# Splitting the stores of the last block: halves by partition, the last one over two DMA queues

## The chip, the cores and the metric

The kernel runs on one core of one Trainium2 chip. Its time is the device time of one execution in microseconds (us); the time before is the median of five runs.

## What is computed

The reference is a light-weight convolution followed by a two-layer block with a leaky ReLU:

```python
def _attn_ref(x, weight):              # x (8, 4096, 192), weight (8 heads, 7 taps)
    w = softmax(weight, axis=-1)       # written out, with 1e-9 in the sum
    x_pad = concat([zeros(6 rows), x], axis=1)
    ...                                # out[b,s,h,g] = sum_k w[h,k] * x_pad[b,s+k,h,g]

def _moe_ref(x, w_in, w_out):          # x (32768, 192), w_in (192, 2048), w_out (2048, 192)
    h = x @ w_in
    g = np.maximum(0.01 * h, h)
    return (g @ w_out).astype(np.float32)
```

The output has 32768 rows of 192 float32 values, 25.2 MB.

## The kernel before

The eight sequences are taken in four pairs, and each pair in blocks of 512 positions, so there are 32 blocks of 2 x 512 rows. For one block: GpSimd's DMAs load x in bf16, SyncE's transposing DMAs put the channels on the partitions, VectorE applies the seven taps (L226, L232), TensorE multiplies by w_in (L494), ScalarE applies the leaky ReLU (L501), and TensorE multiplies by w_out. The second product of a block runs one block late, interleaved with the first product of the next one. The order of each engine's instructions is the order in which the kernel's Python writes them; no scheduler moves them.

The second product comes in two forms. For the blocks in the middle (`mm2_slot`, L574) the result lies transposed in PSUM; `evac_t` (L596) transposes it back on VectorE into a tile `o_t`, and four DMAs store a block (L610). For the first two blocks and for the last one (`mm2_one`, L511) the result comes out with 128 rows of the output on the partitions. The last block has nothing left to be interleaved with, and it is done after the main loop, in eight pieces of 128 rows:

```python
    for n in range(LAST, len(subs)):
        po[n] = psum_o.tile([128, D], FP32, name="po", tag="po")
        for fc in range(NFC):
            mm2_one(None, n, fc, fc == 0, fc == NFC - 1)
        evac_o(n)
```

Each piece is 16 matmuls into a bank of PSUM, then `evac_o(n)`: one copy on VectorE from PSUM into a tile `o_sb` in SBUF (L622), and one store of 128 rows x 768 bytes from SyncE's queue (L625 before). Below, pieces are numbered 1 to 8 and a piece's store has its number. Three things tie these steps to each other:

- Both pools rotate through four buffers (`po` in PSUM, `o_sb` in SBUF). So the copy of piece 5 writes the buffer that store 1 reads, and waits until that store has landed; pieces 6, 7 and 8 wait in the same way for stores 2, 3 and 4.
- The DMAs that SyncE and ScalarE issue signal their landing on eight semaphores, taken in turn, which the built program calls DMAHW0 to DMAHW7. A DMA is issued only when the previous one on its semaphore has landed. SyncE has four stores of `o_t` (L610) just ahead of the last block's stores. They take DMAHW0 to 3, stores 1 to 4 take DMAHW4 to 7, and stores 5 to 8 take DMAHW0 to 3 again.
- After its last store SyncE runs the program's end, which the profile puts on the line of the launch (L745): nine waits one after the other, each for one or two semaphores of DMAs and engines; then all engines meet at a barrier. The nine take the hardware queues' semaphores in this order: none, DMAHW0, 1, 2, 3, 4, 5, 6, 7. In the built program the order is the same before and after the change.

ScalarE issues one DMA in the whole kernel, the load of the convolution's weights at the start (L288). Its last work is the leaky ReLU of the last block.

Of the kernel before, what the change touches and what calls it, by code (L numbers as in the profile page):

```python
# [15 lines left out]
def kernel(  # L16
# [8 lines left out]
    nc = tc.nc  # L25
# [46 lines left out]
    out_rows = out.rearrange("(r s) d -> r s d", r=B)  # L72
# [226 lines left out]
    for sign, off in ((1, 0), (-1, GRP - 1)):  # L299
        nc.gpsimd.affine_select(  # L300
            out=sel[:, :, 0, :], in_=sel[:, :, 0, :], compare_op=mybir.AluOpType.is_ge,
# [42 lines left out]
    for h in range(2):  # L344
        cs = slice(h * NFC // (2 * RUN), (h + 1) * NFC // (2 * RUN))
        nc.gpsimd.dma_start(
            out=w_out.rearrange("p (c i) d -> p c i d", i=RUN)[:, cs],
            in_=moe_w_out.rearrange("(c p i) d -> p c i d", p=128, i=RUN)[:, cs],
# [7 lines left out]
    def warm(n, cols=HT):  # L356
# [10 lines left out]
        out=nmax, in_=w9[:, 0:K], axis=mybir.AxisListType.X,  # L367
# [3 lines left out]
        out=w9[:, 0:K], in_=w9[:, 0:K], func=mybir.ActivationFunctionType.Exp,  # L371
# [61 lines left out]
    for p in range(2):  # L433
# [10 lines left out]
        out=rsum, in0=wml[:, :, K:], scalar=1e-9, in1=whm[:, :, 0, K:],  # L444
# [6 lines left out]
    def act_scale(out, in_, scale):  # L451
# [23 lines left out]
    subs = [  # L475
        (b, e, t0 // 128 + n)
        for b, t0, T in groups[:NSW] for e in range(2) for n in range(T // 128)
    ]
    LAST = len(subs)
# [39 lines left out]
    def mm2_row_slot(q):  # L519

        p, fc = divmod(q, 2 * NFC)
        rnd, fc = divmod(fc, NFC)
        pair = (2 * p, 2 * p + 1)
        first, last = fc == 0, fc == NFC - 1
        if first and rnd == 0:
            for n in pair:
                po[n] = psum_o.tile([128, D], FP32, name="po", tag="po")
        for rt in range(2):  # L530
            ins = mm2_one(
                rt, pair[rt ^ rnd], fc, first and rnd == 0, last and rnd == 1
            )
            if first and rnd == 1:
                sync(ins, seal, "both row tiles have left these banks")
        if last and rnd == 0:
            seal_round(p, ins)
        if last and rnd == 1:
            evac_o(pair[0])

    def seal_round(p, ins):


        nonlocal seal
        if p == 0:
            seal = nc.scalar.copy(out=junk, in_=junk)
        else:
            seal = evac_o(2 * p - 1)
        sync(seal, ins, "between the rounds")
# [65 lines left out]
    def evac_o(n):  # L615
        b, e, s = subs[n]
        rp, st = divmod(b, NB)
        if n % 2 == 0 or n >= LAST:
            osb[n] = o_pool.tile([128, 2, D], FP32, name="o_sb")
        o_sb = osb[n if n >= LAST else n - n % 2]  # L620
        copy = nc.scalar.copy if b < NHALF else nc.vector.tensor_copy
        ins = copy(out=o_sb[:, n % 2, :], in_=po.pop(n))  # L622
        if n >= LAST:
            t0 = st * ST + s * 128
            nc.sync.dma_start(out=out_rows[2 * rp + e, t0 : t0 + 128, :], in_=o_sb[:, n % 2, :])  # L625
        elif n % 2 == 1:
            t0 = st * ST + (s - 1) * 128
            nc.sync.dma_start(
                out=out_rows[2 * rp + e, t0 : t0 + 256, :].rearrange("(c p) d -> p c d", p=128),
                in_=o_sb,  # L630
            )
        return ins
# [21 lines left out]
    for i, grp in enumerate(groups):  # L654
        blk, t0, T = grp
# [10 lines left out]
        for j in range(steps):  # L666
# [41 lines left out]
            if i == NSW and j == steps - 1:  # L708
                evac_o(LAST - 1)
                slot = NSW * NR * NFC  # L710
# [39 lines left out]
```

## Time and profile before

| what | value |
|---|---|
| time, median of 5 runs | 681.69 us (681.49 to 682.32) |
| time of the profiled execution | 681.49 us |
| its span from the first to the last instruction | 679.8 us |
| TensorE busy | 675.8 us, 99% of the span, at the full granted clock |
| VectorE, ScalarE busy | 481.1 us, 518.7 us |
| the last block's second product (L511) | 10.73 us, from 665.87 us |
| the last copy (L622) | 0.36 us, from 676.64 us |
| the last store's issue (L625) | 0.33 us, from 677.02 us |

The span starts at the profile's zero. The difference between the execution's time and its span, 1.69 us, lies outside the instructions. In the timeline a row is: start, duration, engine, line, operation, tiles, count; in brackets the idle time before it and what ended that. An engine's name with a q (SPq, ACTq) means its instruction queue, where DMAs are issued and semaphores waited for; SP is SyncE.

### The profile page before, as it was taken

The page shows a single profiled execution, that of the slowest core. Times are in us where ns is not written, and L with a number is a line of the kernel's source. Part 1 is how long each engine was busy: PE and PEld are TensorE (multiplying, and loading weights), DVE is VectorE, ACT ScalarE, POOL GpSimd, SP SyncE. Part 2 cuts the span into 40 slices and gives each one's busy share as a digit, 9 for nine tenths or more (in the row PEclk, how much of TensorE's full clock was granted, in tenths as well). Part 3 has the DMA queues.
Part 4 walks back from the last instruction along what each step waited for, and adds up shares of the span by engine and source line. Part 5 has one row for each costly group of instructions (what it writes and reads, how often), then busy time and mean ns, then how long its engine had stood idle before and what let it go on. Part 6 is the DMA issues. An engine that isn't in the chain of part 4 may idle for free.

```text
span 679.8 us, 27088 instructions
## 1 busy us (share of the span) xinstructions
PE 675.8 (99%) x12444; PEld 447.7 (66%) x12444; DVE 481.1 (71%) x811; ACT 518.7 (76%) x608; POOL 146.2 (22%) x205
## 2 busy tenths in 40 slices
PE   9999999999999999999999999999999999999998
PEld 6997666666666666666666666666666666666667
DVE  7989467766768666778667687667786676876612
ACT  7899777777777778777777877778777777777781
POOL 7455211122201222211222112222112220000000
PEclk9999999999999999999999999999999999999999
DMA  9999746656647656646556366565665573321123
GB/s 152 92 114 109 55 79 89 83 62 71 91 76 96 72 55 87 92 77 85 65 64 95 75 94 78 56 83 83 88 86 67 59 96 72 72 56 35 32 50 94
DMA packets 213826, 53.27 MB, mean 78 GB/s; under 512 B 209232, under 2 KB 213328, under 8 KB 213712
## 3 DMA queue, kind: packets, MB, share of 16 engines
q0 software_dynamic: 98752, 13.97, 30.4%
q1 hardware_dynamic: 114944, 37.57, 27.4%
q8 instruction: 97, 1.59, 1.0%
q14 instruction: 17, 0.14, 0.1%
q10 hardware_dynamic: 16, 0.00, 0.0%
HBM read 28.31 MB, written 25.17 MB: 79 GB/s over the span
## 4 chain that ended last, share of the span: by engine, by line
PE 99%; DVE 0%; issue 0%
PE ph L494 49%; PE acc L574 44%; PE po L511 5%; PE acc L257 1%; PE warm L358 1%; PE ptr L188 0%; PE ptr L179 0%; DVE o_sb L622 0%; PE warm L394 0%; PE wps L394 0%
## 5 line engine op out<-in xcount | busy, mean ns | idle before, releaser
L501 ACT ACTIVATE g<-ph 128x1024 bf16<-128x1024 f32 x512 | 496.6, 1021 | 140.2 <-PE ph L494 140.0
L232 DVE SCALAR_TENSOR_TENSOR yt<-xt,wk,yt 128x512 bf16<-128x512 bf16 (+1 forms) x582 | 381.0, 724 | 0.2
L494 PE MATMUL ph<-yt,w_in 64*64 64x512 bf16 (+2 forms) x6048 | 377.1, 369 | 0.0
L574 PE MATMUL acc<-g,w_out 64*64 64x512 bf16 x5568 | 339.9, 376 | 0.0
L494 PEld LDWEIGHTS <-w_in 64*64 64x64 bf16 (+1 forms) x6048 | 229.7, 131 | 102.8 <-issue 0.8
L574 PEld LDWEIGHTS <-w_out 64*64 64x64 bf16 x5568 | 178.6, 118 | 118.4
L99 POOL DMA_DIRECT2D x_bf<-in_x_dram x180 | 133.8, 768 | 411.0 <-DMA xt<-x_bf 408.9
L596 DVE STREAM_TRANSPOSE o_t<-acc 128x512 f32<-128x512 f32 x87 | 72.8, 876 | 181.9 <-PE acc L574 181.9
L511 PE MATMUL po<-w_out,g 64*128 64x192 bf16 (+1 forms) x640 | 36.8, 243 | 0.0
L511 PEld LDWEIGHTS <-g 64*128 64x128 bf16 (+1 forms) x640 | 32.6, 95 | 3.2 <-issue 0.4
L226 DVE TENSOR_SCALAR yt<-xt,wk 128x512 bf16<-128x512 bf16 (+1 forms) x97 | 29.8, 335 | 3.2 <-DMA xt<-x_bf 3.1
L584 ACT COPY junk<-junk 128x1 f32<-128x1 f32 x58 | 11.1, 192 | 4.1
L622 DVE COPY o_sb<-po 128x192 f32<-128x192 f32 x8 | 2.8, 356 | 6.8 <-PE po L511 4.2
L257 PE MATMUL acc<-xt,diag 64*64 64x256 bf16 x140 | 5.4, 272 | 0.0
L622 ACT COPY o_sb<-po 128x192 f32<-128x192 f32 x16 | 5.1, 324 | 0.3
L257 PEld LDWEIGHTS <-diag 64*64 64x64 bf16 x140 | 4.3, 106 | 1.4 <-DVE diag L413 0.7
L358 PE MATMUL warm<-const-bfloat16-1.0 128*128 128x512 bf16 (+3 forms) x12 | 4.3, 513 | 0.8 <-PEq L734 0.8
L152 POOL DMA_DIRECT2D x_half<-in_x_dram x6 | 4.3, 730 | 1.0 <-DMA x_rows<-in_x_dram 0.9
L358 PEld LDWEIGHTS <-const-bfloat16-1.0 128*128 128x128 bf16 x12 | 1.5, 138 | 2.5 <-issue 2.5
L148 POOL DMA_DIRECT2D x_rows<-in_x_dram x4 | 2.9, 728 | 0.0
L413 DVE TENSOR_TENSOR diag<-ident,whm 128x448 bf16<-128x448 bf16 (+1 forms) x5 | 2.6, 582 | 0.0
L421 ACT ACTIVATE diag<-ident,whm 128x64 bf16<-128x64 bf16 x10 | 2.5, 336 | 0.0
(47 smaller groups left out, 24.3 us busy)
## 6 DMA issues: line engine op xcount, KB each, us to landing
out_dram<-o_t SPq DMA_DIRECT2D x116, 192.0 KB, 4.6
x_bf<-in_x_dram POOLq DMA_DIRECT2D x180, 64.0 KB, 3.2
out_dram<-o_sb SPq DMA_DIRECT2D x8, 192.0 KB, 3.4
xt<-x_bf SPq DMA_TRANSPOSE x90, 3.8
w_out<-in_moe_w_out_dram POOLq DMA_DIRECT2D x2, 384.0 KB, 8.0
out_dram<-o_sb SPq DMA_DIRECT2D x8, 96.0 KB, 2.0
w_in<-in_moe_w_in_dram POOLq DMA_DIRECT2D x2, 256.0 KB, 4.7
x_nat<-in_x_dram SPq DMA_DIRECT2D x2, 192.0 KB, 2.5
```

The costliest lines, as they stand in the source:

```text
L99: ins = nc.gpsimd.dma_start(out=t[:, c, :, e, :], in_=src[2 * rp + e, :, :, c * CH : (c + 1) * CH],)
L226: lambda s=src, d=dst, c=c: nc.vector.tensor_scalar_mul(d, s, wk[:, c, 0:1])
L232: lambda s=src, d=dst, c=c, k=k: nc.vector.scalar_tensor_tensor(out=d, in0=s, scalar=wk[:, c, k : k + 1], in1=d, op0=mybir.AluOpType.mult, ...
L257: lambda k=k, p=p, a=a, ps=ps, to=to, acc=accs[e * apart]: nc.tensor.matmul(out=acc[to, :T], lhsT=diag[c][ps, p, k, :], rhs=xt[0][ps, c, a ...
L358: nc.tensor.matmul(out=wa[:, 0, 0:cols], lhsT=ones[:, 0:128], rhs=ones[:, 0:cols], start=True, stop=True,)
L494: nc.tensor.matmul(out=ph[m : m + M, e, i * T : (i + 1) * T], lhsT=w_in_of(f, e, c, m, m + M), rhs=y[ps, c, t0 : t0 + T], start=(c == chun ...
L501: act = nc.scalar.activation(out=g[blk][:, nf * u : nf * (u + 1), :, t0 : t0 + T], in_=ph.rearrange("p e (i t) -> p i e t", i=nf), func=my ...
L511: return nc.tensor.matmul(out=po[m], lhsT=g[b][ps, fc, e, s * 128 : (s + 1) * 128], rhs=w_out[ps, fc, :], start=start, stop=stop,)
L574: ins = nc.tensor.matmul(out=acc2[gi, r][e * CH : (e + 1) * CH, 0:T], lhsT=w_out_of(ps, fc, r), rhs=g[b][ps, fc, e, t0 : t0 + T], start=fi ...
L584: seal = nc.scalar.copy(out=junk, in_=junk)
L596: nc.vector.transpose(out=osb[gi, 0][:, 0 : T // GB, :, r], in_=acc2.pop((gi, r))[:, 0:T].rearrange("p (j k) -> p j k", k=GB),)
L622: ins = copy(out=o_sb[:, n % 2, :], in_=po.pop(n))
```

## The change

In the last block, `evac_o` cuts some stores into halves by partition. For pieces 1, 2 and 3 the store becomes two stores of 64 rows, both from SyncE's queue. For piece 8, the last, it becomes two stores of 64 rows, the first half from SyncE's queue and the second from ScalarE's. Pieces 4 to 7 keep one store each. The copies, the matmuls and everything before the last block are the same; 8 stores become 12.

```diff
         if n >= LAST:
             t0 = st * ST + s * 128
-            nc.sync.dma_start(out=out_rows[2 * rp + e, t0 : t0 + 128, :], in_=o_sb[:, n % 2, :])
+            end = n == len(subs) - 1
+            parts = 2 if n < LAST + 3 or end else 1
+            for h in range(parts):
+                ps = slice(h * 128 // parts, (h + 1) * 128 // parts)
+                (nc.scalar if end and h else nc.sync).dma_start(
+                    out=out_rows[2 * rp + e, t0 + ps.start : t0 + ps.stop, :],
+                    in_=o_sb[ps, n % 2, :],
+                )
```

In the built program the stores after the change take the semaphores so: the halves of 1, 2 and 3 DMAHW4 and 5, 6 and 7, 0 and 1; stores 4 to 7 DMAHW2 to 5; of store 8, ScalarE's half DMAHW6 and SyncE's half DMAHW7. The copies of pieces 5, 6 and 7 each wait for two halves where they waited for one store.

## The prediction

> **What bounds the kernel now.** I read the chain that ended last first, since it says which part of the span the edit can touch at all. On the page:
>
> ```profile
> PE 99%; DVE 0%; issue 0%
> PE ph L494 49%; PE acc L574 44%; PE po L511 5%; PE acc L257 1%; PE warm L358 1%; PE ptr L188 0%; PE ptr L179 0%; DVE o_sb L622 0%; PE warm L394 0%; PE wps L394 0%
> ```
>
> TensorE is the chain from end to end. The chain stops at the copy of piece 8, so what comes after is not in it. No instruction ahead of the last block differs, so everything up to about 670 us stays. The question is the tail. The timeline from 676.5 us has it:
>
> ```profile
> 676.27 0.33 PE L511 MATMUL po<-w_out,g 128*128 128x192 bf16 x2
> 676.64 0.36 DVE L622 COPY o_sb<-po 128x192 f32<-128x192 f32 x1 [0.96 <-PE po L511]
> 677.02 0.33 SPq L625 DMA_DIRECT2D out_dram<-o_sb  x1
> ```
>
> The copy ends at 677.00, store 8 is issued 0.02 us later, and the span ends at 679.8. So 2.8 us are left after the last copy, and only these can be shortened. The view of line 625 from 676.9 us gives the store's "DMA to landing" as 1.6 us, so it lands at 678.6. The DMA view of 677.8 to 678.4 us, in 40 slices of 0.015 us, shows its packets:
>
> ```profile
> DMA  0001527488959799887998749263301000000000
> ```
>
> They start in the fourth slice, about 677.85, and end in the 31st, about 678.26: 0.42 us. So the store's 1.6 us are 0.83 before the first packet, 0.42 of packets and 0.35 until SyncE knows. What follows is the program's end (L745). Its waits on SyncE, asked for in two windows, 677.3:678.6 and 678.62:678.95:
>
> ```profile
> L745 SPq EVENT_SEMAPHORE  x4: 28/28/28, 677.4 to 677.6; - x4
> ```
>
> ```profile
> L745 SPq EVENT_SEMAPHORE  x5: 28/28/28, 678.7 to 678.9; - x5
> ```
>
> Four of the nine waits are passed while the store is still on its way. The fifth is the one for DMAHW3, store 8's semaphore. It holds SyncE, 1.0 us by the view of waits ("SPq L745 <- DMA out_dram<-o_sb: 1.0, 1, 1.0"), and four more come after it, for stores landed long before. Windows of 0.05 us show one of the five starting each 0.06 us. So after the landing SyncE spends 4 x 0.06 = 0.24 us on waits that have nothing to wait for, and then the barrier.
>
> **Part one: the semaphores.** Three more stores ahead of store 8 move the rotation on by three, and the fourth extra DMA is store 8's own second half. The halves of store 8 now signal DMAHW6 and 7, and these are the last two of the nine waits. The seven before them are passed while the halves are on their way: 7 x 0.06 = 0.42 us, against the 1.2 us between the end of issue (677.36) and the landing. After the landing one wait is left if both land together, 0.06 us, or none if ScalarE's half is first. So 0.24 - 0.06 = 0.18 us is saved, up to 0.24. I take 0.18. This gain is the sure one: it follows from order alone.
>
> **Part two: store 8 in two halves.** The 0.83 us before the first packet is not per row. The first o_t store is another shape (512 runs of 384 bytes) and its issue takes 0.32 us against 0.33 here, so half the rows should not shorten it. The 0.42 us of packets could at best be halved if two queues feed the DMA engines twice as fast: -0.21 us. The busy share in the row above reads 7 to 9 tenths in the middle, so the engines are nearly full there and little can be fed faster. Against it stands the only place where both queues issue together, the kernel's start:
>
> ```profile
> 0.81 0.60 ACTq L288 DMA_DIRECT2D w<-in_weight_dram  x1
> 0.81 0.96 SPq L145 DMA_DIRECT2D x_nat<-in_x_dram  x2
> ```
>
> There ScalarE's issue took 0.60 us, which is 0.27 more than store 8's 0.33, and SyncE's two took 0.96 with a gap, some 0.45 each. If the later half pays the same, the landing is 0.27 us later. The bounds are therefore -0.21 and +0.27, and I take 0: the rows at both ends are about equally far from this store. ScalarE is idle when it is asked: its last leaky ReLU ends before 666, and its half waits for DMAHW6 (the first half of store 2, landed by about 674.5) and for the copy. So nothing is queued behind it but the barrier.
>
> The Trainium skill, page "DMA: Bandwidth & Descriptors", section "Rules for kernel authors", speaks against this part: for two transfers to disjoint partition halves it says "Don't bother", since both halves run on the same 16 DMA engines and serialize. By that rule the gain of the halves is nothing and the sum is part one alone; by the best reading of the row it would be 0.21 us more.
>
> **Part three: three more issues on SyncE.** Stores 1 to 4 are issued at 670.50, 671.65, 672.56 and 673.05 and take 1.06, 0.81, 0.40 and 0.40 us; the first two are slow while the o_t stores' data drains (their own issues grow from 0.32 to 1.13 us). The gaps between issues are about 0.1 us. Each extra half costs at least one more short issue with its gap, 0.33 + 0.1 = 0.43 us; part of it falls into the time when the queue is full anyway. Three make 1.3 us at the low price. At the high price a half costs what its whole costs now: 1.06 + 0.81 + 0.40 + 3 x 0.1 = 2.57 us. I take 1.3, since the issues are short as soon as the drain is over. Two things must absorb this:
>
> ```profile
> 674.39 0.62 DVE L622 COPY o_sb<-po 128x192 f32<-128x192 f32 x2 [2.61 <-DMA out_dram<-o_sb]
> ```
>
> The copy of piece 5 already waits 2.61 us for store 1 to land (670.50 + 3.8 = 674.3). That wait is off the path: TensorE has four banks and never writes a ninth piece, so a late copy delays no matmul. What counts is the copy of piece 8, which needs store 4 landed. Store 4 is issued at 673.05 and takes 2.0 to land, at 675.05; TensorE frees the copy at 676.64. The slack is 1.6 us, and 1.3 fits. The other cover is SyncE's queue: stores 5 to 7 are issued at 674.78, 675.20 and 675.70, the last done at 676.08, and store 8 needs the queue at 677.02, so 0.94 us is free. Stores 4 and 5 gate these: with 1.3 us store 4's issue ends at 674.75, just as store 5 wants the queue. So part three is hidden: 0. Without that cover it would cost what exceeds 1.6 us.
>
> The semaphores' reuse adds waits too: store 4 now needs the third o_t store landed, and store 5 the fourth. The DMA view gives a median of 4.8 us for these, issued at 668.49 and 669.27, so 673.3 and 674.1; both are ahead of the time when those stores are issued anyway. Cost 0.
>
> **The sum.** -0.18 + 0 + 0 = about -0.2 us. The profiled execution took 681.49, so it would take 681.3, with a span of 679.6. That execution was the fastest of the five; the median lies 0.2 above it, and the forecast for the median is 681.69 - 0.2 = 681.5 us. This is 0.03%. A measurement of this kernel can tell about 0.2% from no change, 1.36 us, so I forecast no change.
>
> **The rivals.**
>
> - The halves overlap fully: two queues feed the engines at once, the packets take 0.21 us, and ScalarE's half lands first. Then -0.24 - 0.21 = -0.45, 681.2 us. For it: the fill and the drain of the packet row take part of its 0.42 us. Against: its middle is nearly full.
> - The two queues hinder each other as at the start: +0.27 - 0.18 = +0.1, 681.8 us. For it: the 0.60 us issue. Against: two DMAs stood on SyncE there.
> - Slower: store 4 comes so late that the copy of piece 8 waits for it. Price: at 2.57 us, store 4 lands at 677.6 instead of 675.05, the copy starts at about 677.7 instead of 676.64, everything after moves by 1.05 us, less 0.2: 682.5 us. It decides once the three halves cost SyncE more than 1.6 us together. To be slower by over 0.2% they would have to cost 1.6 + 1.36 + 0.2 = 3.2 us. Against it: the issues of 0.40 us from 672.56 on.
> - The change does not do what it says: ScalarE's half signals or starts late and the semaphores' order saves nothing. Then about 681.7.
>
> A gain of over 0.2% would need half of the 2.8 us after the last copy, and no mechanism here reaches a quarter of it.
>
> **How the numbers follow.** My forecast (part one alone, halves neutral) 0.45; full overlap 0.2; the queues hinder each other 0.15; the late store 4 0.1; no effect 0.1. All five lie within 0.2%; what is left over is the spread of executions (681.49 to 682.32, 0.12%) and a late store that costs more than I allow. Hence 0.04 faster, 0.90 same, 0.06 slower. The range: down from full overlap, 681.2, by 0.3, since the fastest of the five runs lies 0.2 below their median and five are few, 680.9; up to the late store, 682.5, which also takes in the slowest of the five runs less 0.2.
>
> **What would show it.** In the profile after: seven of SyncE's waits at L745 before the landing and two after it; 2.6 us from the end of the last copy to the end of the span; ScalarE's issue of about 0.3 to 0.6 us at 677.0; the copy of piece 8 at 676.64 still freed by TensorE, not by a DMA. I am wrong if the copy of piece 8 waits for a store, if the last half lands later than 1.6 us after its issue, or if TensorE's matmuls at L511 take other than 10.7 us.

## The result, and the profile after

The changed kernel takes 682.43 us (median of 25 runs), the kernel before 681.60 us (45 runs). The medians differ by 0.83 us, slower; the ratio of the means is 1.0011, 95% interval 1.0006 to 1.0017. It is small, inside the 0.2% that was called no change, and clear of noise, on the other side of the forecast. The profiled execution took 682.33 us, its span 680.6 us.

The page's chain that ended last, by engine and by line, after the change:

```profile
PE 98%; DMA 1%; SPq 0%; ACT 0%; DVE 0%; issue 0%; DVEq 0%
PE ph L494 49%; PE acc L574 44%; PE po L511 4%; PE acc L257 1%; DMA out_dram<-o_sb 1%; PE warm L358 0%; SPq L629 0%; ACT xt L199 0%; PE ptr L188 0%; DVE o_sb L622 0%; PE ptr L179 0%; PE wps L394 0%; DVEq L622 0%
```

Before, TensorE was the chain to its end. Now the chain has stores of `o_sb` and SyncE's queue in it. The same chain from 660 us on, in order of time (start, duration, what):

```profile
670.36 1.06 SPq L629
...
672.59 0.54 SPq L629
...
673.17 3.81 DMA out_dram<-o_sb x2
...
677.11 0.36 DVE o_sb L622
```

The last copy is no longer freed by TensorE. It waits for a store, and that store stands behind the halves in SyncE's queue. The timeline says the same:

```profile
677.11 0.36 DVE L622 COPY o_sb<-po 128x192 f32<-128x192 f32 x1 [0.20 <-DMA out_dram<-o_sb]
677.50 0.55 ACTq L629 DMA_DIRECT2D out_dram<-o_sb  x1
```

SyncE's issues one by one (the timeline of SP, one window for each): the second half of store 1, both of store 2, both of store 3, and store 4.

```profile
671.46 1.03 SPq L629 DMA_DIRECT2D out_dram<-o_sb  x1
672.59 0.54 SPq L629 DMA_DIRECT2D out_dram<-o_sb  x1
673.17 0.59 SPq L629 DMA_DIRECT2D out_dram<-o_sb  x1
673.87 0.54 SPq L629 DMA_DIRECT2D out_dram<-o_sb  x1
674.46 0.59 SPq L629 DMA_DIRECT2D out_dram<-o_sb  x1
675.15 0.53 SPq L629 DMA_DIRECT2D out_dram<-o_sb  x1
```

The halves of stores 2 and 3, 64 rows each, take longer to issue (0.54 to 0.59 us) than the whole store 3 did before:

```profile
672.56 0.40 SPq L625 DMA_DIRECT2D out_dram<-o_sb  x1
```

Two rows are something else. Store 1's second half takes 1.03 us, while the o_t stores' data is still draining, and store 4, which is whole, takes 0.53 behind a half.

The last store's two halves show "DMA to landing us min/median/max: 1.9/2.0/2.1", where the whole store showed 1.6. SyncE's half is the one that lands after 1.87 us, ScalarE's lands after 2.12. The DMA share from 678.4 to 679.4 us, in slices of 0.025 us, has the packets of both:

```profile
DMA  0000000003439479496556576795945311000000
```

Up to 678.89 the view counts packets of SyncE's queue alone. SyncE's first packet comes at 678.62, 1.13 us after the issue, and ScalarE's at 678.90, 1.40 us after it. A whole store took 0.83. Last, SyncE's waits of the program's end (L752 now), in the windows 678:679.6 and 679.6:679.76:

```profile
L752 SPq EVENT_SEMAPHORE  x7: 28/28/28, 678.0 to 678.6; - x7
L752 SPq EVENT_SEMAPHORE  x2: 28/28/28, 679.6 to 679.7; - x2
```

Seven before the landing and two after it, as forecast.

So the time can be split. Nothing before the last block differs, and still the copy of piece 1 starts at 667.33 us here and at 667.47 before; over all runs below it starts between 667.30 and 668.08. The rows, before and after:

```profile
667.47 0.36 DVE L622 COPY o_sb<-po 128x192 f32<-128x192 f32 x1
```

```profile
667.33 0.36 DVE L622 COPY o_sb<-po 128x192 f32<-128x192 f32 x1
```

I therefore count from that copy, which takes this spread out:

| stretch | before | after | difference |
|---|---|---|---|
| start of copy 1 to start of copy 8 | 9.17 | 9.78 | +0.61 |
| issue of store 8 until SyncE passes the wait for it | 1.63 | 2.14 | +0.51 |
| from there to the end of the span | 1.13 | 0.96 | -0.17 |
| start of copy 1 to the end of the span (the tail) | 12.32 | 13.27 | +0.95 |

Copy and wake-up between are the same. The tail's 0.95 less the 0.14 of earlier start is the 0.8 us by which the span grew.

### The profile page after: what moved, and what is told of

It is laid out like the page before. It is cut to its first block, busy times and chain, and to the rows that moved or that the text cites. A ratio compares the mean times of both kernels' runs of the same rounds, so it can differ in the third digit from the quotient of the medians.

```text
span 680.6 us, 27096 instructions
## 1 busy us (share of the span) xinstructions
PE 675.4 (99%) x12444; PEld 446.7 (66%) x12444; DVE 481.9 (71%) x811; ACT 518.8 (76%) x608; POOL 146.7 (22%) x205
## 4 chain that ended last, share of the span: by engine, by line
PE 98%; DMA 1%; SPq 0%; ACT 0%; DVE 0%; issue 0%; DVEq 0%
PE ph L494 49%; PE acc L574 44%; PE po L511 4%; PE acc L257 1%; DMA out_dram<-o_sb 1%; PE warm L358 0%; SPq L629 0%; ACT xt L199 0%; PE ptr L188 0%; DVE o_sb L622 0%; PE ptr L179 0%; PE wps L394 0%; DVEq L622 0%
```

## Experiments: which part costs what

The theory from this profile: the halves of stores 1 to 3 hold up store 4 and with it the copy of piece 8 (+0.6), the halves of store 8 land late (+0.5), the order of waits gives back 0.17. The rivals: two queues at once hinder each other; any three more DMAs cost this; the waits at the end are worth nothing. The times of each run stand with runs of the kernel before on the same chip; the tails are from the traces.

**Only the last store split.** `parts = 2 if end else 1`

> Only store 8 is split, over SyncE's and ScalarE's queues; stores 1 to 7 stay whole. If the loss has two parts, a late copy of piece 8 (0.6 us) and a late landing of the two halves (0.5 us), this keeps the second alone: the copy of piece 8 is freed by TensorE again, the last half lands 2.1 us after its issue instead of 1.6, and the kernel is 0.4 to 0.5 us slower than before. If the halves in SyncE's queue are the whole of it, the landing comes back to 1.6 us and the time is that of before, 0.06 us less for one wait fewer at the end.

682.19 us against 681.52, ratio 1.0009, interval 1.0000 to 1.0017. The tail is 12.91, +0.59.

```profile
677.09 0.36 DVE L622 COPY o_sb<-po 128x192 f32<-128x192 f32 x1 [0.96 <-PE po L511]
```

```profile
DMA to landing us min/median/max: 1.9/2.1/2.2
```

The copy is TensorE's again, the late landing stays. The second part exists alone. The tail's 0.59 is a little over the 0.4 to 0.5 that was expected.

**Only the first three split.** `parts = 2 if n < LAST + 3 else 1`

> Stores 1 to 3 are split, store 8 is whole on SyncE. With two parts of the loss: the copy of piece 8 waits for store 4 and starts 0.6 us later, store 8 lands 1.6 us after its issue, one wait follows instead of four (-0.18 us), in sum 0.4 us slower than before. If the two queues are the whole of the loss, the copy is on time and the kernel is 0.18 us faster than before.

682.13 us against 681.52, ratio 1.0009, interval 1.0000 to 1.0018. The tail is 12.66, +0.34, as expected; the whole time moved by 0.6, with an interval that holds both.

```profile
677.03 0.36 DVE L622 COPY o_sb<-po 128x192 f32<-128x192 f32 x1 [0.20 <-DMA out_dram<-o_sb]
```

Copy 1 is at 667.35 here, so copy 8 comes after 9.68. Store 8, whole again, lands after 1.6. The two parts' tails add up: 0.59 + 0.34 = 0.93, against 0.95 for the whole change.

**The order of the waits alone.** In the first two blocks four stores become two each, so the rotation moves on by four:

```diff
-            nc.sync.dma_start(out=out_rows[...].rearrange("(c p) d -> p c d", p=128), in_=o_sb)
+            parts = 2 if n >= LAST - 8 else 1
+            for h in range(parts):
+                cs = slice(h * 2 // parts, (h + 1) * 2 // parts)
+                nc.sync.dma_start(out=out_rows[...].rearrange(...)[:, cs], in_=o_sb[:, cs])
```

> The last block's stores are those of before; four stores of the first two blocks go in two halves by column of rows (128 rows each), which moves the rotation of semaphores on by four, so that store 8 signals DMAHW7, the last wait of the nine. If the order of the waits is worth what the prediction gave it, nothing but the barrier follows the landing: 0.24 us faster than before, eight waits ahead of the landing and one after it in the profile. If the waits at the end cost nothing, no difference.

The waits (L748) in the windows 677.4:678.7 and 678.7:678.82:

```profile
L748 SPq EVENT_SEMAPHORE  x8: 28/28/28, 677.5 to 677.9; - x8
L748 SPq EVENT_SEMAPHORE  x1: 28/28/28, 678.8 to 678.8; - x1
```

The tail is 12.09, -0.23: the size is right. The whole time does not show it: 681.63 against 681.52, ratio 1.0003, interval 0.9994 to 1.0012. A gain of 0.03% is below what these runs resolve, so it is shown in the trace alone.

## Experiments: two queues, or the half itself

**Store 8 whole on ScalarE's queue.** `(nc.scalar if n == len(subs) - 1 else nc.sync).dma_start(...)` in the kernel before.

> No store is split; store 8 goes whole to ScalarE's queue. If a half of 64 rows is slow by its form (in the changed kernel its first packet comes 1.1 us and more after the issue, where whole stores take 0.83), this whole store on the other queue has its first packet 0.83 us after its issue and lands after 1.6 us: the time of before. If ScalarE's queue is the slow one, it lands 0.3 to 0.5 us later and the kernel loses that.

681.54 us against 681.58, ratio 1.0000, interval 0.9991 to 1.0009. ScalarE's issue and its landing:

```profile
L625 ACTq DMA_DIRECT2D out_dram<-o_sb x1: 382/382/382, 677.1 to 677.1; - x1
...
DMA to landing us min/median/max: 1.7/1.7/1.7
```

ScalarE's queue is not slow: 0.05 us more issue than SyncE's, and its first packet comes 0.88 us after the issue instead of 0.83.

**Store 8 in halves of 64 rows, both on SyncE.** `parts = 2 if end else 1`, and `nc.sync` for both.

> Only store 8 is split, in halves of 64 rows, both on SyncE's queue. If the form is slow, the first half's first packet comes 1.2 us after its issue, as with two queues, the second half follows 0.64 us after the first as those of stores 2 and 3 do, and it lands 2.5 us after the copy: 0.8 us slower than before. If the two queues hinder each other, one queue frees the first half: its first packet comes after 0.83 us, and the second lands 2.1 us after the copy at most.

682.59 us against 681.58, ratio 1.0017, interval 1.0007 to 1.0026; the tail +0.93. The first half is issued at 676.86 and takes 0.56 us on a queue of its own. The DMA engines' busy share from 678 to 679.2 us, in slices of 0.03 us:

```profile
DMA  0033396939722100000000005376797842100000
```

The first packet comes at 678.07, 1.2 us after the issue, with no other queue at work. So a half is slow to start by itself. The pair of queues can still add to it; the next run has both queues without the 64 rows.

**Store 8 in halves by column over both queues.** Each half keeps 128 rows and has 384 bytes of each.

```diff
-                ps = slice(h * 128 // parts, (h + 1) * 128 // parts)
+                ds = slice(h * D // parts, (h + 1) * D // parts)
...
-                    in_=o_sb[ps, n % 2, :],
+                    in_=o_sb[:, n % 2, ds],
```

> Only store 8 is split, by column, 128 rows of 384 bytes each, over SyncE's and ScalarE's queues. If the form of 64 rows is slow and the queues do not hinder each other, both first packets come 0.83 us after the issue and the later half lands after 1.6 us: the time of before. If the two queues hinder each other, the later half's first packet comes 0.3 us or more after the other's, and it lands after 2.0 us or more.

681.63 us against 681.58, ratio 1.0002, interval 0.9993 to 1.0011; the tail 12.40, +0.08. The timeline, and the DMA share from 677.8 to 678.4 us in the slices of 0.015 us in which the prediction showed the whole store:

```profile
677.06 0.33 SPq L629 DMA_DIRECT2D out_dram<-o_sb  x1
677.06 0.38 ACTq L629 DMA_DIRECT2D out_dram<-o_sb  x1
```

```profile
DMA  0000002456788999999997998799886665231000
```

Both halves together are on the engines from 677.90 to 678.36, 0.46 us, where the whole store took 0.42. SyncE's first packet comes 0.84 us after its issue and ScalarE's 0.99, 0.15 us behind it, where ScalarE alone was 0.05 behind. So the two queues hinder each other by some 0.1 us, and they gain nothing either: the later half lands after 1.68 us. The rival is small here and not nothing. In the change ScalarE's half started 0.28 us behind SyncE's, and how much of this is the pair is open, as a half of 64 rows on ScalarE's queue alone was not run. The Trainium skill's page "DMA: Bandwidth & Descriptors", section "Rules for kernel authors", says of partition halves that they serialize on the same 16 engines; here neither cut gains, and the cut by partition loses 0.5 us besides.

**Stores 1 to 3 in halves by column.** As many DMAs as in the change, all on SyncE, store 8 whole.

> Stores 1 to 3 go in two halves by column, 128 rows of 384 bytes each, on SyncE; store 8 is whole. As many DMAs as with the halves by partition. If 64 rows are what makes a half dear, the issues after the first two take 0.33 to 0.40 us instead of 0.54 to 0.60, store 4 lands by about 676.0 at the latest, the copy of piece 8 is freed by TensorE, and the kernel is 0.18 us faster than before (one wait after the landing). If three more DMAs are the cost whatever their form, the copy of piece 8 is 0.5 us late again and the kernel 0.3 us slower.

681.37 us against 681.58, ratio 0.9997, interval 0.9988 to 1.0007; the tail 12.13, -0.19. The issues and the last copy:

```profile
672.45 0.39 SPq L629 DMA_DIRECT2D out_dram<-o_sb  x1
672.88 0.43 SPq L629 DMA_DIRECT2D out_dram<-o_sb  x1
...
676.52 0.36 DVE L622 COPY o_sb<-po 128x192 f32<-128x192 f32 x1 [0.61 <-PE po L511]
```

The copy is TensorE's again, 9.17 us after copy 1. Store 4's issue starts 7.01 us after copy 1 instead of 5.58, so these three extra halves cost 1.43 us together, under the slack of 1.6. Three more DMAs are hidden, as the prediction had it, when they are as quick as these. The rival "any three more DMAs" falls.

## Experiments: is it the buffer that makes the copy late?

**Eight buffers for `o_sb`.** A pool of its own, `o8_pool`, with `bufs=8`; the rest as in the change.

> The changed kernel with eight buffers for o_sb instead of four, so no copy of the last block waits for a store. If the copy of piece 8 is late only because store 4 lands late, it starts at 676.5 us again; SyncE's queue is then the next limit: its issues end at about 677.05, 0.2 us after the copy, so 0.4 us of the 0.8 lost come back. If SyncE's queue with its three more issues is the limit anyway, the time stays at 0.8 us over before.

685.51 us against 681.52, ratio 1.0060, interval 1.0047 to 1.0072: a miss of both expectations. The view of waits on SP:

```profile
SPq L630 <- DMA out_dram<-o_sb: 4.0, 1, 4.0
```

In this build ScalarE's half of store 8 took its place in the rotation ahead of store 4. SyncE's store 4 then waited 4.0 us for a half issued at 677.15. The copy of piece 8 was on time here (9.24 us after copy 1, freed by TensorE), but the time cannot be compared. The test was spoilt, and it showed another cost that two queues on one set of semaphores can have.

**The same with one queue.** Stores 1 to 3 in halves of 64 rows, store 8 whole, eight buffers.

> Stores 1 to 3 in halves of 64 rows as in the change, store 8 whole on SyncE, and eight buffers for o_sb, so no copy of the last block waits for a store. If the copy of piece 8 is late only because its buffer waits for store 4, it starts right after TensorE, about 9.17 us after the copy of piece 1 as before the change, where with four buffers it was 9.68. SyncE's queue is then next: with issues of 0.54 to 0.60 us for the halves it is free about 0.2 us after the copy, which the order of the waits (-0.18) gives back: no difference to before. If the queue itself were what held the end, the time would be as with four buffers, 0.3 us or more over before.

```profile
676.80 0.36 DVE L623 COPY o_sb<-po 128x192 f32<-128x192 f32 x1 [0.96 <-PE po L512]
...
677.39 0.40 SPq L630 DMA_DIRECT2D out_dram<-o_sb  x1
```

(The first line is from VectorE's timeline, the second from SP's.) With copy 1 at 667.56, copy 8 comes after 9.24, 0.07 later than before, and is TensorE's: the wait was for the buffer. Its end is 677.16, and SyncE issues store 8 only at 677.39, 0.2 us late, so the queue is the next limit, as expected. The tail is 12.49, +0.17; expected was about 0. The whole time, 681.96 against 681.52, ratio 1.0007, interval 0.9998 to 1.0016, does not tell these apart.

## Experiments: what is slow about 64 rows

**Even and odd rows.** `ps = slice(h, 128, parts)`: 64 partitions, spread over all 128, both halves on SyncE.

> Only store 8 is split, into the even and the odd rows, 64 partitions each spread over all 128, both on SyncE. If the slow packets of the halves (0.047 us against 0.035) come from 64 neighbouring partitions sharing half of the ports, as the Trainium skill's page 'DMA: Bandwidth & Descriptors', section 'The descriptor swizzle', suggests with its engines 0 to 7 for partitions 0 to 63, the packets take 0.035 us here. If the slow issue and first packet (0.56 and 1.2 us) come from the count of 64, they stay; if from the place of the rows, they go back to 0.33 and 0.83.

One execution, 682.60 us. The issue of the first half, and the DMA share from 678.4 to 679.5 us:

```profile
677.30 0.56 SPq L629 DMA_DIRECT2D out_dram<-o_sb  x1
```

```profile
DMA  0000357897442000000000000003369795331000
```

Two separate costs. The packets take 0.035 us each by the trace's records, as in whole stores, where 64 neighbouring rows take 0.047; this agrees with what the expectation drew from the section it names, though no run here shows the ports. The slow issue and the first packet after 1.2 us stay.

**Other counts.** Store 8 cut at row 96, at 80, and at 32, both parts on SyncE; then 64 rows in two runs each. Each of the four kernels was executed once (682.11, 682.46, 682.35 and 682.68 us), so only the rows of the traces are used.

> Only store 8 is split, into 96 and 32 rows, both on SyncE. Asked is how issue and first packet go with the number of rows: whole stores of 128 rows take 0.33 us and 0.83 us, halves of 64 rows 0.56 and 1.2. If fewer rows are dearer step by step, 96 rows lie between (0.4 us and 1.0 us) and 32 rows above 0.56; if anything but 128 rows takes a slower way, 96 rows take about 0.56 and 1.2 too.

> Only store 8 is split, into 80 and 48 rows, both on SyncE. So far 128 and 96 rows take 0.33 to 0.35 us to issue and 0.84 us to the first packet, 64 rows 0.56 and 1.2. If there is a threshold between 64 and 96 rows, 80 rows fall clearly on one side and 48 rows are at least as slow as 64. If 64 is a case of its own, 80 and 48 are both fast.

> Only store 8 is split, into 32 and then 96 rows, both on SyncE, so that the 32 rows are issued to a free queue. Behind 96 rows they took 0.42 us to issue and 0.92 to the first packet. If few rows are slow, they are at least as slow as 64 here (0.56 and 1.2); if 64 is a case of its own, they take 0.33 and 0.84.

> Only store 8 is split, into halves of 64 rows on SyncE, and each row is stored as two runs of 368 bytes with a gap of 16 bytes, so that a half has 128 runs instead of 64; 8 of the 192 columns of the last 128 rows are left out. If the number of runs decides, the issue takes 0.33 to 0.40 us and the first packet comes after 0.84; if the 64 partitions decide, it stays at 0.56 and 1.2.

The issues in SP's timeline: 96 rows, 32 behind them; 80, 48 behind them; 32, 96 behind them; and the first half of 64 rows in two runs.

```profile
677.39 0.35 SPq L629 DMA_DIRECT2D out_dram<-o_sb  x1
677.79 0.42 SPq L629 DMA_DIRECT2D out_dram<-o_sb  x1
```

```profile
677.63 0.35 SPq L629 DMA_DIRECT2D out_dram<-o_sb  x1
678.03 0.42 SPq L629 DMA_DIRECT2D out_dram<-o_sb  x1
```

```profile
677.37 0.34 SPq L629 DMA_DIRECT2D out_dram<-o_sb  x1
677.77 0.41 SPq L629 DMA_DIRECT2D out_dram<-o_sb  x1
```

```profile
677.18 0.64 SPq L629 DMA_DIRECT2D out_dram<-o_sb  x1
```

The first packets come 0.85 us after the issue for the first 96, 80 and 32 rows, about 0.92 for the parts behind them, and 1.29 for the 64 rows in two runs. So 32, 48 (on a free queue in the next run), 80, 96 and 128 rows are quick to issue and to start, and 64 are not, whether the rows lie side by side or apart and whether the half has 64 runs or 128. It is not fewer rows that are dear, nor a threshold. Why the count of 64 is slow stays open.

**The change with its cut moved to row 48.** Everything else as changed: twelve stores, two queues, the same semaphores.

```diff
-                ps = slice(h * 128 // parts, (h + 1) * 128 // parts)
+                ps = slice(0, 128) if parts == 1 else (slice(0, 48), slice(48, 128))[h]
```

> The change as it is, with its twelve stores, its queues and its semaphores, but each split store is cut at row 48 instead of row 64 (48 and 80 rows). If the count of 64 is what costs, the parts issue in 0.35 to 0.42 us, the copy of piece 8 is freed by TensorE again (9.17 us after the copy of piece 1), the last part lands 1.7 us after its issue, one wait is left after it, and the time is 0.1 to 0.2 us under before, 0.9 to 1.0 under the change. If splitting by partition costs whatever the count, or the two queues hinder each other, the time stays 0.5 us or more over before.

681.58 us against 681.77, ratio 0.9997, interval 0.9988 to 1.0006; the tail 12.33, that of before.

```profile
676.93 0.36 DVE L622 COPY o_sb<-po 128x192 f32<-128x192 f32 x1 [0.46 <-PE po L511]
677.32 0.38 ACTq L629 DMA_DIRECT2D out_dram<-o_sb  x1
```

The copy is on time and the loss is gone, with 16 rows moved from one half to the other. On a free queue the 48 rows take 0.33 us to issue and 0.83 to the first packet. The gain of the order of waits is eaten by the landing: 1.80 us after the issue instead of 1.63. ScalarE's first packet comes 0.13 us behind SyncE's here. On SyncE alone, in the cut at row 80 above, 80 rows landed 1.58 us after their issue and 48 rows 1.60, so this lateness comes with the second queue. Of part two's 0.51 us, 0.34 go with the count of 64 and 0.17 stay. Of the copy's 0.61 nothing is left. Splitting store 8 by partition is still no help, but nearly all of the loss was the 64.

**A version to beat both: four stores by column.** `parts = 2 if n < LAST + 4 else 1`, by column, store 8 whole on DMAHW7.

> A version meant to beat both: stores 1 to 4 in halves by column (128 rows of 384 bytes) on SyncE, store 8 whole on SyncE, where it now signals DMAHW7, the last of the waits. The halves by column cost 0.38 to 0.43 us of issue each, the copy of piece 8 is freed by TensorE, eight waits are passed ahead of the landing and one after it: 0.24 us faster than before. If one more half makes store 4 or SyncE's queue late, the copy of piece 8 or store 8's issue moves by 0.2 us or more and nothing is gained.

681.62 us against 681.52, ratio 1.0000, interval 0.9991 to 1.0009.

```profile
677.14 0.36 DVE L622 COPY o_sb<-po 128x192 f32<-128x192 f32 x1 [0.59 <-DMA out_dram<-o_sb]
```

The second expectation held: store 4 itself now goes in halves and lands late, the copy comes after 9.33 instead of 9.17, and the tail is 12.24, -0.08. The shortest tails are those of the order of waits alone (12.09) and of three by column (12.13), 0.23 and 0.19 under before; the times of both are not told apart from before.

## Why the prediction was wrong, step by step

What bounds the kernel, the tail of 2.8 us and the absence of any mechanism of 0.2% were right. The sign was wrong. Two of the things by which the prediction said it would be wrong came true: the copy of piece 8 waits for a store, and the last half lands later than 1.6 us after its issue.

- Part one, the order of the waits: right. -0.18 forecast; -0.17 in the change, -0.23 with the rotation alone moved by four.
- Part two, store 8 in two halves, taken at 0 between -0.21 and +0.27: +0.51 measured, outside its bounds. The reasoning "half the rows should not shorten it" looked only for a saving. The row it rested on, 512 runs from 32 partitions issued in 0.32 us, was read as showing that the start does not depend on the shape. It depends on it at 64. The rival that the two queues hinder each other, read from 0.60 us of ScalarE's first issue, priced this at 0.27, about half of what came, and mostly for a wrong cause: ScalarE alone took 0.38, and one queue alone had the same slow start. Cut at row 48, two queues still cost 0.17; the other 0.34 is the 64.
- Part three, three more issues, taken at 1.3 us between 1.3 and 2.57: store 4's issue starts 7.82 us after copy 1 (675.15 - 667.33) instead of 5.58 (673.05 - 667.47), 2.24 later. The slack was counted as 1.6; 2.24 - 1.6 = 0.64, and the copy moved by 0.61. The path and the slack were right, and the term that failed is the price of a half: 0.43 us each was taken, from whole stores. From issue to issue store 1 took 1.08 us more in two halves than whole (2.23 against 1.15), since its second half still fell into the drain, store 2 took 0.37 more and store 3 0.79. Not all of the 2.24 is the 64: with quick halves the three cost 1.43 (by column) and 1.49 (cut at row 48), store 1 the most again. So the sum of 1.3 would have been nearly right for these; what took it past 1.6 are mainly the halves of 64 rows in stores 2 and 3, at 0.54 to 0.59 an issue.
- The rival "slower", store 4 late, was the case that came true, with 0.1 for its chance and 682.5 us for its time. Its decision point, 1.6 us for three halves, was passed. Its price left out part two: it had 1.05 for the copy where 0.61 came, and nothing for the landing where 0.51 came. That its 682.5 lies so near the measured 682.43 is luck: two errors cancel.

The step as a whole: both parts priced a shape that the trace of before does not have by the rows of other shapes, and took the favourable end once and the middle once. The reason given for the favourable end, issues that are short once the drain is over, held for whole stores, and did not cover store 1's second half, which is issued before that.

## What to carry to other kernels

Splitting a DMA does not split its price: an issue and a start are paid for each part, and a shape not yet in the trace has to be timed before it is put on a queue with little slack. When a store goes in parts, follow whoever waits for its buffer, and whoever stands behind it in its queue, down to the last copy. At the end of a program the order in which landings are waited for is worth a look: a last store that signals the last wait saved some 0.2 us of the tail here.

## What was not expected of the hardware

- A store of 64 partitions takes 0.56 us to issue on a free queue and 1.2 us to its first packet, against 0.33 to 0.35 and 0.83 to 0.85 for 32, 48, 80, 96 and 128 partitions.
- Packets of 768 bytes from 64 neighbouring partitions take 0.047 us, those of 64 partitions spread over all 128 take 0.035, as in a whole store.
- When SyncE and ScalarE issue the two parts of a store at once, ScalarE's first packet comes behind SyncE's: by 0.15 us for halves by column, 0.13 for 48 and 80 rows, 0.28 for 64 and 64. ScalarE alone was 0.05 behind.
- Two queues that share one rotation of semaphores can hold each other up: 4.0 us in one build.
